# Reordering the opening of the row stage of a spectral-mixer training kernel, one forward bank from the other PSUM ring, and the last moves on three queues

## The chip, the cores and the metric

The kernel runs as one program on one core of a Trainium2 chip. The metric is device time in microseconds (us), the median of several executions; lower is better. A profile of one further execution gives every instruction's start and duration on the core's engines: PE (TensorE, matrix products; its weight loads are listed apart as PEld), DVE (VectorE), ACT (ScalarE), POOL (GpSimd) and SP (SyncE, which here only issues DMA transfers).

## The reference

The kernel computes the forward pass of one block and all its gradients (inputs and outputs bf16, x and grad_out [1, 2048, 448]):

```python
def _A_ref(x, w_r, w_i):                      # spectral filter
    X = rfft2(x.astype(float32), axes=(-2, -1))
    X = X * (w_r + 1j * w_i)
    return irfft2(X, s=(2048, 448), axes=(-2, -1)).astype(bfloat16)

def _B_ref(x, w1, b1, w2, b2):                # MLP over the 2048 tokens
    h = _layernorm(x)
    u = gelu(einsum("bsd,sf->bdf", h, w1) + b1)
    return (einsum("bdf,fs->bds", u, w2) + b2).transpose(0, 2, 1)

h  = x + _A_ref(_layernorm(x), w_r, w_i)
h2 = h + _B_ref(_layernorm(h), w1, b1, w2, b2)
out, vjp = jax.vjp(f, x, w_r, w_i, w1, b1, w2, b2);  grads = vjp(grad_out)
```

## The kernel before, in words

All work is in tiles of 128 partitions. Fourier transforms are matrix products with tables of sines that the kernel makes itself. The 2048 rows are split as 16 x 128: a *row stage* transforms the 128-long part of the rows and the 448 columns (`row_a`, `row_b`), a *spectral stage* (`s2_stage`) does the 16-long part forward, the filter, and the 16-long part back, and `inv_rows` goes back to rows and columns. The sections that the change touches lie in the first 95 us; the MLP, its gradients and the backward spectral pass follow.

**Order.** PE, SP, DVE and ACT run their instructions in the order in which the Python code emits them; POOL alone is ordered by the build. So what is emitted ahead of something on the same engine delays it.

**Weight-gradient matmuls as filling.** `dg_gen` (line 828) computes W2 @ grad_out: 14 blocks j of 16 matmuls (j, t), 128x448 each, into one `ps_mm` bank per block. `fill(n)` (792) emits n of them between other work; FILL_A and FILL_B (908, 909) say how many at each step t, and `drain()` the rest. Blocks 0 to 4 of W2 are turned on PE (`turn_w2`, 314): transposes into PSUM, copied out by ACT, called from inside `dg_gen` (block 4 after matmul (3, 4)); later blocks are turned by DMA.

**PSUM.** There are two rings of four banks, `ps_ff` (177) and `ps_mm` (180).

**Who copies out of PSUM.** `evac` (184) picks ACT or DVE by a running account of estimated work (`Meter`, 53; costs in lines 64 to 71).

**The row stage (871 to 951).** Layernorm statistics (`ln_stats`, 806) of the tiles of x; their reciprocal standard deviation by ACT's Sqrt and a DVE reciprocal (tiles 0 to 3), by nine small Newton steps on DVE (`rstd_of`, 849; tiles 4 and 5) or the like on POOL. `fold_prep` or `fold_quarters` fold a pair of tiles on DVE; `scale_R` puts the row's factor into the matrix R; `row_a(t)` (660) is four matmuls with it into one `ps_ff` bank, copied out to `blks`. `row_b(h)` (670) is four matmuls with the table `csF` into another bank; after each odd h a DMA, the *move*, lays the result out anew as D2. Step t runs `row_a(t + 1)`, then filling, `scale_R(t + 3)`, `row_b(t - 3)`, a fold, statistics, and steps of `gen_UV` (479), which makes the tables U and V.
`gen_RT` (523) makes R transposed by one matmul from four rearranged copies of R (903 to 907); `inv_rows` is its first user. `defer` (204) issues a DMA only after 1.1 us of PE work (RESH_LAG) have been emitted.

**The spectral stage (696).** Five rounds s. `four` (699) does 48 small matmuls into four banks: forward for s < 4, back for the round before. Forward results are copied by ACT, multiplied on DVE with the filter, transformed back, copied, and moved to D3 by DMA (730, 731); the last four moves gate `inv_rows` (756), whose `first` needs D3 and R transposed, and whose copies `aT` feed the second product. Its consumer `h_consumer` (988) forms h and its statistics.

**SP's queue.** It issues x, grad_out and W2 loads first (331 to 346), among them `gtail`, a tail of grad_out of 16 x 64, then two small bias loads (`load_biases`, 813), the filter's loads (`w_io`), the moves, and, after the spectral stage, the chunks of W2 and W1 for the MLP (1024 to 1028). `load_w1c` fills a ring of three; the third lies where W2's block 13 lay.

Of the kernel before, what the change touches and what calls it, by code (L numbers as in the profile page):

```python
# [124 lines left out]
def kernel(  # L125
# [188 lines left out]
    def turn_w2(j, parts=((0, 8), (8, 8))):  # L314
        for h, n in parts:
            pt = (ps_mm if j < 2 else ps_ff)()[:].bitcast(BF16).rearrange("p (t c) -> p t c", c=P)
            for t in range(n):
                nc.tensor.transpose(pt[:, t, :], w2n[j][:, h + t, :], ident[:])
            sc.copy(out=w2Ts[j][:, h:h + n, :], in_=pt[:, 0:n, :])
# [26 lines left out]
    nc.sync.dma_start(out=gtail[:, 0:64], in_=grad_out[0][S - 16:S, 3 * P:D])  # L346
# [261 lines left out]
    resh = [nc.sync]  # L608
# [51 lines left out]
    def row_a(t, R):  # L660
        pa = ps_ff()
        ft = folds[t // 2]
        for k in range(4):
            o = DC * (4 * (t % 2) + k)
            mm(pa[:, k * P:(k + 1) * P], lhsT=ft[:, o:o + P], rhs=R, start=True, stop=True)
        if t % 4 == 0:
            blks[t // 4] = blk_ring.next()
        evac(out=blks[t // 4][:, :, t % 4, :], in_=pa[:].rearrange("p (n x) -> p n x", x=8))

    def row_b(h, quarters=None):  # L670
        u, e, c = h // 4, h // 2 % 2, h % 2
        if h < 0 or h >= NT:
            return
        pd = ps_ff()
        pv = pd[:, 0:452].rearrange("p (c k) -> p c k", c=2)
        pq = pd[:, 0:452].rearrange("p (c e k) -> p c e k", c=2, e=2)
        for w in (1, 0):
            for b in range(2):
                n = 4 * (4 * (2 * w + b) + 2 * c + e)
                lhsT = blks[u][0:DC, n:n + 4].rearrange("p i j x -> p (i j x)")  # L680
                if quarters is not None:
                    mm(pq[:, 1 - w, b, :], lhsT=lhsT, rhs=quarters[0:DC, w, b, 0:KW // 2], start=True, stop=True)
                    continue
                mm(pv[:, 1 - w, :], lhsT=lhsT, rhs=csF[0:DC, w, b, :], start=(b == 0), stop=(b == 1))
        if c == 0:
            css[h // 2] = cs_ring.next()
        cs = css[h // 2]
        if quarters is not None:
            evac(out=cs[:, c].rearrange("p w (j e) -> p w e j", e=2), in_=pq)
        else:  # L690
            evac(out=cs[:, c], in_=pv)
        if c:
            defer(RESH_LAG, lambda: resh[0].dma_start(out=D2[u:u + 125:4, 8 * e:8 * e + 8].rearrange("p g c k -> p (g c k)"),
                                                      in_=cs.rearrange("p x c k -> p (x c k)")), cs)

    def s2_stage(get_x, on_mult, n1, n2, gap, after=None, scale=None, split=False):
        flush()

        def four(tables, s, turn, rhs):
            gs = set_groups(s)  # L700
            ps = [ps_ff()[:, 0:452].rearrange("p (c k) -> p c k", c=2) for _ in gs]
# [10 lines left out]
        for s in range(5):  # L712
# [8 lines left out]
            if s:  # L721
                for a, pv in enumerate(four((VTt, UTt, UTn), s - 1, -1, lambda a, g, r: y[blk(r), a])):
# [7 lines left out]
                    eng = nc.sync if split and s == 4 and a > 1 else gp_  # L730
# [82 lines left out]
    def load_biases():  # L813
        gp_.memset(smr, 0.0)
        nc.sync.dma_start(out=smr[0:NFB, 0, :], in_=B_b1.rearrange("(j p) -> j p", p=P))
# [88 lines left out]
    for c in range(2):  # L904
        for e in range(2):
            sc.copy(out=Rp.rearrange("p (e a q b c) -> p c e a q b", e=2, c=2, q=8, a=2)[:, c, e],
                    in_=Rm[:, 64 * c + 32 * e:64 * c + 32 * e + 32].rearrange("p (q a b) -> p a q b", q=8, a=2))
    FILL_A = (4, 4, 8, 12, 6, 3, 3, 3, 3, 3, 3, 3, 3, 3, 3, 3)
    FILL_B = (0, 0, 2, 2, 2, 2, 4, 4, 3, 2, 2, 2, 2, 2, 2, 2)
    for t in range(NT):  # L910
        if t == 0:
            load_w2T()
        if t + 1 < NT:
            row_a(t + 1, Rs.pop(t + 1))
        fill(FILL_A[t])
        if 1 <= t and t + 3 < NT:
            if t + 3 in (4, 8, 12):
                while Meter.side:
                    Meter.side.pop(0)()
            Rs[t + 3] = scale_R(t + 3)  # L920
# [28 lines left out]
        if t == 2:  # L949
# [11 lines left out]
    while held_w2:  # L961
        held_w2.pop(0)()
    fill(14)
# [6 lines left out]
    drain()  # L970
# [7 lines left out]

    assert not pending
# [8 lines left out]
    def h_consumer(s1, py):  # L988
# [3 lines left out]
        if s1 >= 1:  # L992
# [32 lines left out]
    w1cs = [load_w1c(jp) for jp in range(3)]  # L1025
# [426 lines left out]
```

## Time and profile before

| | us |
|---|---|
| runs | 342.69, 340.54, 342.59; median 342.59 |
| the profiled execution | 340.96 |
| its span, first to last instruction | 339.2 |
| PE idle in the span | 8.9 |
| granted TensorE clock | 0.999 |

Busy us by stretch, from the same profile (span's start is 0):

| stretch | PE | DVE | ACT | POOL |
|---|---|---|---|---|
| 6.47 to 19.35, opening up to row_b(0) | 11.25 of 12.88 | 12.12 | 11.11 | 9.95 |
| 19.35 to 32.84, up to row_a(10) | 12.36 of 13.49 | 13.17 | 9.27 | 7.07 |
| 32.84 to 49.20, end of the row stage | 16.36 of 16.36 | 10.39 | 11.42 | 5.86 |
| 49.20 to 76.11, spectral stage | 26.50 of 26.91 | 16.77 | 17.77 | 8.33 |
| 76.11 to 92.85, inverse rows | 16.34 of 16.74 | 13.10 | 15.47 | 3.82 |

How to read it: a timeline row gives start, duration, engine, source line, operation, the tile written and read, the form, and in brackets how long the engine was idle just before and what ended that. Most instructions are recorded by a helper, so L84 is any DVE or ACT operation, L220 a matmul, L225 a small one. A row merges equal neighbours (x4). A waits line gives engine and line, what it waited for, total us, times, longest. A windows line gives, for a stretch, its length, then the busy time of PE, PEld, DVE, ACT and POOL with the number of instructions, the granted clock, the DMA share and GB/s. Matmul ends are modelled, so "busy" can hide short waits between starts; a 448-column matmul that waits for nothing starts 0.187 us after the one before.

### The profile page before, as it was taken

The page shows a single profiled execution, that of the slowest core. Times are in us where ns is not written, and L with a number is a line of the kernel's source. Part 1 is how long each engine was busy: PE and PEld are TensorE (multiplying, and loading weights), DVE is VectorE, ACT ScalarE, POOL GpSimd, SP SyncE. Part 2 cuts the span into 40 slices and gives each one's busy share as a digit, 9 for nine tenths or more (in the row PEclk, how much of TensorE's full clock was granted, in tenths as well). Part 3 has the DMA queues.
Part 4 walks back from the last instruction along what each step waited for, and adds up shares of the span by engine and source line. Part 5 has one row for each costly group of instructions (what it writes and reads, how often), then busy time and mean ns, then how long its engine had stood idle before and what let it go on. Part 6 is the DMA issues. An engine that isn't in the chain of part 4 may idle for free.

```text
span 339.2 us, 7995 instructions
## 1 busy us (share of the span) xinstructions
PE 330.3 (97%) x2893; PEld 174.0 (51%) x2893; DVE 252.6 (74%) x678; ACT 206.2 (61%) x447; POOL 83.9 (25%) x255
## 2 busy tenths in 40 slices
PE   8898999999999999999999999999999999999995
PEld 4565665456545555555555555555334344555552
DVE  8999649726947888594226988787598984599994
ACT  6886766858965544523132346665488875688882
POOL 7755602331310000000001111210002222156660
PEclk9999999999999999999999999999999999999999
DMA  7979999949999999787986989636998999969785
GB/s 250 399 195 183 228 245 196 167 110 261 252 366 305 337 277 241 179 259 197 187 192 154 188 176 165 171 83 203 262 254 280 184 227 281 349 164 295 233 309 198
DMA packets 136142, 78.03 MB, mean 230 GB/s; under 512 B 86568, under 2 KB 127512, under 8 KB 135976
## 3 DMA queue, kind: packets, MB, share of 16 engines
q1 hardware_dynamic: 133576, 73.59, 82.6%
q0 software_dynamic: 2528, 3.95, 5.5%
q8 instruction: 22, 0.36, 0.5%
q14 instruction: 16, 0.13, 0.2%
HBM read 28.33 MB, written 22.04 MB: 149 GB/s over the span
## 4 chain that ended last, share of the span: by engine, by line
PE 85%; DVE 6%; ACT 3%; DMA 2%; SPq 2%; issue 1%; POOL 0%; DVEq 0%; ACTq 0%
PE ps_mm L220 73%; PE ps_ff L220 8%; PE ps_ff L225 4%; DMA rA<-in_A_x_dram 2%; ACT rO L84 2%; DVE r L84 2%; DVE stats L84 1%; SPq L329 1%; SPq L310 1%; DVE rS L84 1%; DVE rA L84 1%; ACT rAT L84 0%; DVE rD L84 0%; DVE rX L84 0%; DVE rB L84 0%
## 5 line engine op out<-in xcount | busy, mean ns | idle before, releaser
L220 PEld LDWEIGHTS <-r 128*128 128x128 bf16 (+2 forms) x628 | 58.4, 104 | 47.6 <-issue 3.0
L220 PEld LDWEIGHTS <-rS 128*128 128x128 bf16 (+1 forms) x468 | 36.3, 97 | 33.4 <-issue 7.7
L84 ACT CAST rO<-ps_mm 128x512 bf16<-128x512 f32 (+1 forms) x69 | 36.9, 584 | 14.6 <-PE ps_mm L220 13.0
L220 PE MATMUL ps_mm<-rD,r 128*128 128x448 bf16 x224 | 44.5, 352 | 0.0
L220 PEld LDWEIGHTS <-rst 128*128 128x128 bf16 (+1 forms) x320 | 23.6, 97 | 31.3 <-issue 14.0
L731 POOL DMA_DIRECT2D r<-r x30 | 17.8, 601 | 66.5 <-ACT r L84 59.3
L220 PE MATMUL ps_mm<-rC,rE 128*128 128x448 bf16 x144 | 32.1, 353 | 0.5 <-DMA rC<-in_grad_out_dram 0.4
L220 PE MATMUL ps_mm<-rB,r 128*128 128x448 bf16 x160 | 31.2, 352 | 0.1
L220 PE MATMUL ps_mm<-rG,rst 128*128 128x512 bf16 (+1 forms) x128 | 28.7, 380 | 0.2 <-ACT rO L84 0.2
L220 PE MATMUL ps_mm<-r,rst 128*128 128x512 bf16 (+2 forms) x144 | 27.4, 345 | 0.0
L84 ACT ACTIVATE r<-ps_mm,rstd_h 128x448 bf16<-128x448 f32 x16 | 10.1, 633 | 26.8 <-PE ps_mm L220 26.8
L84 ACT CAST r<-ps_ff 128x452 bf16<-128x452 f32 x43 | 23.2, 589 | 4.5 <-PE ps_ff L225 2.1
L84 DVE SCALAR_TENSOR_TENSOR r<-ps_mm,b2col,r 128x448 bf16<-128x448 f32 x16 | 10.9, 682 | 19.9 <-PE ps_mm L220 19.8
L84 ACT ACTIVATE r<-rC 128x448 bf16<-128x448 bf16 x16 | 9.1, 571 | 26.7 <-DMA out_dram<-r 14.1
L1189 POOL TENSOR_SCALAR lcol<-lcol 128x1 f32<-128x1 f32 x16 | 8.5, 528 | 64.7 <-ACT r L84 64.7
L84 ACT ACTIVATE rG<-rG 128x896 bf16<-128x896 bf16 x14 | 13.3, 950 | 14.9 <-DVE rG L84 14.7
L220 PEld LDWEIGHTS <-rO 128*128 128x128 bf16 (+1 forms) x165 | 15.3, 98 | 12.2 <-ACT rO L84 0.2
L84 ACT CAST rS<-ps_ff 128x512 bf16<-128x512 f32 x31 | 18.1, 587 | 2.5 <-PE ps_ff L220 2.4
L220 PE MATMUL ps_ff<-csI,rAT 113*128 113x224 bf16 (+1 forms) x108 | 19.0, 298 | 0.4 <-ACT rAT L84 0.2
L84 DVE TENSOR_SCALAR rG<-rG 128x896 bf16<-128x896 bf16 x28 | 10.9, 388 | 10.0 <-ACT rG L84 10.0
L220 PE MATMUL ps_mm<-rC,rO 128*128 128x448 bf16 x80 | 18.1, 353 | 0.0
L84 ACT CAST rG<-ps_mm 128x512 bf16<-128x512 f32 (+1 forms) x28 | 13.8, 534 | 6.8 <-PE ps_mm L220 6.7
(202 smaller groups left out, 638.2 us busy)
## 6 DMA issues: line engine op xcount, KB each, us to landing
out_dram<-rO SPq DMA_DIRECT2D x34, 256.0 KB, 3.0
r<-in_B_w_dram SPq DMA_DIRECT2D x5, 1024.0 KB, 8.4
r<-r POOLq DMA_DIRECT2D x30, 113.0 KB, 5.4
out_dram<-rG SPq DMA_DIRECT2D x11, 256.0 KB, 3.7
r<-r SPq DMA_DIRECT2D x12, 226.0 KB, 2.5
r<-in_B_w_dram SPq DMA_DIRECT2D x3, 896.0 KB, 5.1
rS<-in_B_w_dram SPq DMA_DIRECT2D x3, 896.0 KB
rB<-in_B_w_dram SPq DMA_DIRECT2D x5, 512.0 KB, 9.8
```

What stands on the lines that cost most here:

```text
L84: fn(**kw)
L220: nc.tensor.matmul(out, lhsT=lhsT, rhs=rhs, start=start, stop=stop)
L225: nc.tensor.matmul(out, lhsT=lhsT, rhs=rhs, start=start, stop=stop)
L310: nc.sync.dma_start(out=w2n[j], in_=B_w2[j * P:(j + 1) * P, :].rearrange("f (t c) -> f t c", c=P))
L329: nc.sync.dma_start(out=go_tp[:, 4 * q:4 * q + 4, :], in_=go_tp_d[:, 4 * q:4 * q + 4, :])
L731: defer(RESH_LAG, lambda g=g, ab=ab, eng=eng: eng.dma_start(out=D3[rowbase(g):rowbase(g) + 29:4, :, :, :], in_=ab), ab)
L1189: gp_.tensor_scalar(out=m1, in0=ms, scalar1=-1.0 / D, scalar2=None, op0=ALU.mult)
```

## The change

In the opening: the statistics and Sqrt of tiles 2, 3 are emitted ahead of the first W2 copies; row_a(0) to row_a(3) are run before the loop and copied by ACT whatever the account says, the latter two late (`late_a`); tiles 4, 5 take Sqrt and reciprocal in place of the Newton steps, with their fold and scalings right behind; the sine of the forward table comes before the loop. In the loop: row_a(8) is copied by ACT, the second copy of W2's block 4 comes after it (`late_c`); one step of `gen_UV` is taken before the statistics of t = 1 and none at t = 6; R transposed is made at t = 13, not t = 2. The last row move goes at once on ACT's DMA queue. The gtail and bias loads go behind the row stage. In the spectral stage the fourth bank of each forward group is a `ps_mm` bank; the last four D3 moves go on POOL, SP, ACT, SP (before: POOL, POOL, SP, SP). After it 18 filling matmuls are run in place of all the rest, so that the last of them stand in `inv_rows`, and the third W1 chunk is loaded from `h_consumer`.

```diff
-            sc.copy(out=w2Ts[j][:, h:h + n, :], in_=pt[:, 0:n, :])
+            (Later(sc, late_c) if j == 4 and h else sc).copy(out=w2Ts[j][:, h:h + n, :], in_=pt[:, 0:n, :])
...
-    nc.sync.dma_start(out=gtail[:, 0:64], in_=grad_out[0][S - 16:S, 3 * P:D])
...
-    def row_a(t, R):
+    def row_a(t, R, how=None):
...
-        evac(out=blks[t // 4][:, :, t % 4, :], in_=pa[:].rearrange("p (n x) -> p n x", x=8))
+        (how or evac)(out=blks[t // 4][:, :, t % 4, :], in_=pa[:].rearrange("p (n x) -> p n x", x=8))
...
         if c:
-            defer(RESH_LAG, lambda: resh[0].dma_start(...), cs)
+            eng = nc.scalar if h == NT - 1 and quarters is csQ else nc.sync
+
+            def move():
+                eng.dma_start(...)
+            if eng is nc.scalar:
+                move()
+            else:
+                defer(RESH_LAG, move, cs)
...
-            ps = [ps_ff()[:, 0:452].rearrange("p (c k) -> p c k", c=2) for _ in gs]
+            ps = [(ps_mm if split and turn > 0 and a == 3 else ps_ff)()[:, 0:452].rearrange("p (c k) -> p c k", c=2)
+                  for a in range(4)]
...
-                    eng = nc.sync if split and s == 4 and a > 1 else gp_
+                    eng = (gp_, nc.sync, nc.scalar, nc.sync)[a] if split and s == 4 else gp_
...
     def load_biases():
         gp_.memset(smr, 0.0)
+        nc.sync.dma_start(out=gtail[:, 0:64], in_=grad_out[0][S - 16:S, 3 * P:D])
...
-    turn_w2(0, ((0, 4), (4, 4)))
-    row_a(0, Rs.pop(0))
     for t in range(2, 4):
         ln_stats(xn, t, mvx)
     sc.activation(out=rstd_x[:, 2:4], in_=mvx[:, 2:4, 1], func=ACT.Sqrt, bias=eps_x, scale=1.0)
+    turn_w2(0, ((0, 4), (4, 4)))
+    row_a(0, Rs.pop(0), sc.copy)
     turn_w2(0, ((8, 8),))
+    row_a(1, Rs.pop(1), sc.copy)
     fold_prep(xn, 1)
+    ve.reciprocal(out=rstd_x[:, 2:4], in_=rstd_x[:, 2:4])
+    Rs.update({t: scale_R(t) for t in range(2, 4)})
+    late_a, late_c = [], []
     cs_ops = []
     gen_fwd_d(cs_ops)
-    ve.reciprocal(out=rstd_x[:, 2:4], in_=rstd_x[:, 2:4])
-    Rs.update({t: scale_R(t) for t in range(2, 4)})
...
-    fill(4)
+    fill(3)
+    for t in range(2, 4):
+        row_a(t, Rs.pop(t), Later(sc, late_a).copy)
+    fill(1)
     for t in (4, 5):
         ln_stats(xn, t, mvx)
-    for fn in rstd_of(4, 6):
+    sc.activation(out=rstd_x[:, 4:6], in_=mvx[:, 4:6, 1], func=ACT.Sqrt, bias=eps_x, scale=1.0)
+    fold_prep(xn, 2)
+    ve.reciprocal(out=rstd_x[:, 4:6], in_=rstd_x[:, 4:6])
+    Rs.update({t: scale_R(t) for t in range(4, 6)})
+    sc.activation(out=warm, in_=half_r, func=ACT.Sin, scale=1.0 / 64.0)
+    cs_ops.pop(0)()
+    for fn in late_a:
         fn()
-    fill(0)
-    turn_biases, place_biases = load_biases()
...
-    for c in range(2):
-        for e in range(2):
-            sc.copy(out=Rp.rearrange(...)[:, c, e], in_=Rm[:, 64 * c + 32 * e:64 * c + 32 * e + 32].rearrange(...))
...
+    def uv_step():
+        for _ in range(3):
+            if next(uv, None):
+                break
...
-        if t + 1 < NT:
-            row_a(t + 1, Rs.pop(t + 1))
+        if 4 <= t + 1 < NT:
+            row_a(t + 1, Rs.pop(t + 1), sc.copy if t == 7 else None)
+        if t == 7:
+            late_c.pop()()
         fill(FILL_A[t])
-        if 1 <= t and t + 3 < NT:
+        if 3 <= t and t + 3 < NT:
...
         if t % 2 and t < 12:
-            if t // 2 + 2 < 2 * U_Q:
+            if t == 1:
+                pass
+            elif t // 2 + 2 < 2 * U_Q:
...
         if t == 1:
-            sc.activation(out=warm, in_=half_r, func=ACT.Sin, scale=1.0 / 64.0)
             while cs_ops:
                 cs_ops.pop(0)()
+            uv_step()
         for i in STATS.get(t, ()):
             ln_stats(xn, i, mvx)
-        for _ in range(3 if t > 0 else 0):
-            if next(uv, None):
-                break
+        if t not in (0, 1, 6):
+            uv_step()
...
-        if t == 2:
+        if t == 13:
+            for c in range(2):
+                for e in range(2):
+                    sc.copy(out=Rp.rearrange(...)[:, c, e], in_=Rm[:, 64 * c + 32 * e:64 * c + 32 * e + 32].rearrange(...))
             gen_RT()
...
     while held_w2:
         held_w2.pop(0)()
+    turn_biases, place_biases = load_biases()
     fill(14)
...
-    drain()
+    fill(18)
...
-    assert not pending
...
-        if s1 >= 1:
+        if s1 == 0:
+            w1cs.append(load_w1c(2))
+        else:
             square_h(s1 - 1)
...
-    w1cs = [load_w1c(jp) for jp in range(3)]
+    w1cs = [load_w1c(jp) for jp in range(2)]
```

More of the change, by code (lines that the diff above doesn't have):

```diff
@@ L606 @@
     D3 = cut(r3, 0, NT, 2, KW)
-    resh = [nc.sync]
     def rowbase(s_):
@@ L692, in row_b @@
         if c:
-            defer(RESH_LAG, lambda: resh[0].dma_start(out=D2[u:u + 125:4, 8 * e:8 * e + 8].rearrange("p g c k -> p (g c k)"),
-                                                      in_=cs.rearrange("p x c k -> p (x c k)")), cs)
+            eng = nc.scalar if h == NT - 1 and quarters is csQ else nc.sync
+            def move():
+                eng.dma_start(out=D2[u:u + 125:4, 8 * e:8 * e + 8].rearrange("p g c k -> p (g c k)"),
+                              in_=cs.rearrange("p x c k -> p (x c k)"))
+            if eng is nc.scalar:
+                move()
+            else:
+                defer(RESH_LAG, move, cs)
     def s2_stage(get_x, on_mult, n1, n2, gap, after=None, scale=None, split=False):
@@ L903 @@
     W_AT = {0: 2, 1: 1, 2: 2, 3: 1, 4: 2, **{t: 1 for t in range(5, 11)}, 11: 4}
-    for c in range(2):
-        for e in range(2):
-            sc.copy(out=Rp.rearrange("p (e a q b c) -> p c e a q b", e=2, c=2, q=8, a=2)[:, c, e],
-                    in_=Rm[:, 64 * c + 32 * e:64 * c + 32 * e + 32].rearrange("p (q a b) -> p a q b", q=8, a=2))
     FILL_A = (4, 4, 8, 12, 6, 3, 3, 3, 3, 3, 3, 3, 3, 3, 3, 3)
     FILL_B = (0, 0, 2, 2, 2, 2, 4, 4, 3, 2, 2, 2, 2, 2, 2, 2)
+    def uv_step():
+        for _ in range(3):
+            if next(uv, None):
+                break
     for t in range(NT):
@@ L948 @@
             gen_inv_s(INV_S[t])
-        if t == 2:
+        if t == 13:
+            for c in range(2):
+                for e in range(2):
+                    sc.copy(out=Rp.rearrange("p (e a q b c) -> p c e a q b", e=2, c=2, q=8, a=2)[:, c, e],
+                            in_=Rm[:, 64 * c + 32 * e:64 * c + 32 * e + 32].rearrange("p (q a b) -> p a q b", q=8, a=2))
             gen_RT()
```

## The prediction

> **What bounds the kernel now.** I read the page first (busy shares, chain of waits), then the waits of the tensor engine, then the timelines of the stages that the diff touches.
>
> ```profile
> span 339.2 us, 7995 instructions
> PE 330.3 (97%) x2893; PEld 174.0 (51%) x2893; DVE 252.6 (74%) x678; ACT 206.2 (61%) x447; POOL 83.9 (25%) x255
> PE 85%; DVE 6%; ACT 3%; DMA 2%; SPq 2%; issue 1%; POOL 0%; DVEq 0%; ACTq 0%
> ```
>
> PE is busy for 97%, and no matmul is removed. All that can be won is time in which PE waits: 8.9 us idle, plus waits that hide inside modelled "busy" time. The profiled execution took 340.96 us (span 339.2 and 1.8 around it), 1.63 below the median of 342.59; I sum against it and add the difference back.
>
> The waits of PE in the first 46 us, and the rows around the two long ones:
>
> ```profile
> PE ps_ff L220 <- DVE rS L84: 1.8, 2, 1.0
> PE ps_mm L220 <- DMA rC<-in_grad_out_dram: 0.4, 1, 0.4
> PE ps_mm L318 <- DMA rB<-in_B_w_dram: 0.3, 1, 0.3
> ```
> ```profile
> 14.26 0.54 PE L220 MATMUL ps_mm<-rC,rE 128*128 128x448 bf16 x2
> 15.57 0.65 PE L220 MATMUL ps_ff<-rX,rS 128*128 128x128 bf16 x4 [0.78 <-DVE rS L84]
> ...
> 28.88 0.92 PE L220 MATMUL ps_mm<-rC,rO 128*128 128x448 bf16 x4
> 30.81 0.38 PE L220 MATMUL ps_ff<-rX,rS 128*128 128x128 bf16 x4 [1.01 <-DVE rS L84]
> ```
> ```profile
> 12.01 0.18 DVE L84 TENSOR_SCALAR mvx<-mvx 128x2 f32<-128x2 f32 x1
> ...
> 13.64 0.16 DVE L84 SCALAR_TENSOR_TENSOR rstd_x<-nt_f,rstd_x 128x2 f32<-128x2 f32 x1
> ...
> 15.13 0.69 DVE L84 TENSOR_TENSOR rS<-rA 128x448 bf16<-128x448 bf16 x2
> ...
> 30.08 0.68 DVE L84 CAST rS<-ps_ff 128x512 bf16<-128x512 f32 x1
> ```
>
> row_a(4) (15.57) waits for the fold at 15.13, which stands behind nine tiny Newton steps (12.01 to 13.80: 1.79 us). row_a(9) (30.81) waits for the copy of row_a(8), late on a full DVE (13.17 us busy of the 13.49 between 19.35 and 32.84). 448 columns pass in 0.187 us back to back, so the true losses are the starts less that: 1.2 us at row_a(4) (0.25 of it inside the group), 1.18 at row_a(9), 0.28 at row_a(10).
>
> **The opening, part by part.** *ACT.* The Sqrt of tiles 2, 3 now stands ahead of the first W2 copies and waits for statistics that end at 7.56. By the start-to-start times of its rows (0.48 us for 512 elements, 0.93 for 1024) the copies follow at 7.76, and the first weight-gradient matmul goes from 8.19 to 8.38. row_a(1)'s copy also comes before the copies of the second W2 block; that block's first copy ends at 11.2, so matmuls (1, 0..3) start there, not at 10.48. Most of this is covered: the next group waits anyway for the second quarter of grad_out (landed 11.67). It starts at 11.97 rather than 11.71, and with row_a(2), row_a(3) and the RT product out of the way (0.22, 0.22, 0.06) matmul (1, 4) starts at 12.72 against 12.69.
> *DVE.* Nine Newton steps go (-1.79 us), a reciprocal comes (0.16), Sqrt goes to ACT, and fold 2 and both scalings come directly behind the statistics: ready at 13.5. Ten matmuls after 12.72, row_a(4) starts at 14.6 instead of 15.57, without its inner 0.25: -1.2. The third W2 block lands at 15.29, so its transposes wait 0.1. The planner's balance (costs of lines 64 to 71, summed by hand; for the kernel before it gives the split that the trace shows) now sends row_b(0)'s copy to DVE, behind which row_b(1) finds its bank 0.2 late. Opening: -1.0 (bounds +0.3, if ACT's longer queue shows in full, and -1.2).
> *Late copies.* row_a(2) and row_a(3) keep their two banks until ACT has done Sqrt, Sin table (1.28) and the first basis: to about 15.7. row_a(4) and the next transposes still find the banks of row_a(0) and (1); cost nothing, 0.9 us if a bank is missing (one 1024 copy).
>
> **The middle.** Three table steps (17.73 to 19.43 before) now run on DVE while x's third quarter is in flight (landed 16.42), so with the Newton steps gone DVE is 1.2 us ahead at t = 3. row_a(8) goes to ACT (0.6 off DVE), and the sine of V, which ACT awaited for 2.76 us with the W2 copies behind it, comes one step later. So row_a(9) waits no more; the second fold behind row_a(10) ends 1.2 + 0.6 earlier, at 31.0, while PE could be there at 30.2. row_a(10): 32.84 to 31.0, so **-1.8** for all up to here. Bounds: -1.0 (opening alone) and -2.8 (DVE no longer last).
>
> **The RT product** moves to t = 13, behind four copies that ACT does only after the copy of the inverse table:
>
> ```profile
> 11.65 0.60 ACT L84 COPY rO<-Rm 128x32 bf16<-128x32 bf16 x4
> ```
> ```profile
> 41.52 0.37 ACT L84 CAST UVT<-ps_ff 128x256 bf16<-128x256 f32 x1 [0.51 <-PE ps_ff L225]
> ```
>
> Before, this lay 2 us ahead of its use. Now the copies end at 41.52 + 0.3 + 0.6 = 42.4, and PE, in order, stands at the product from 41.34 with two W2 matmuls and row_a(15) queued behind it: **+1.05** (0.3 if the table's copy goes to DVE, 1.3 with a slower hand-over). No cover: PE is the last engine here.
>
> **The end of the row stage.** The last move goes to ACT's queue at once (some 0.6 us of ACT, as an issue on SP; the csI copies behind it have 1.5 us of room). The planner puts row_b(12) and (13) both on ACT, so the move that the first spectral group needs (issued 44.98, landed 49.00, group at 49.20) is some 0.4 late: **+0.2** (0 to 0.5). Three tiny loads leave SP's early queue, so the W2 and filter loads behind them are issued earlier; those in front land as before: 0. In their new place they delay W2 transposes by about 1 us of 5 us room: 0.
>
> **The spectral stage.** Widths of the eight groups of small matmuls; the narrowest is the floor:
>
> ```profile
> 49.20:49.91 0.71, 0.71 (x50) 0.51 (x49) 0.00 (x0) 0.00 (x0) 0.00 (x0) 1.00 0.91 199
> 60.39:61.32 0.93, 0.93 (x50) 0.53 (x49) 0.83 (x3) 0.71 (x2) 0.00 (x0) 1.00 1.18 266
> 65.45:66.74 1.29, 0.94 (x49) 0.42 (x49) 1.19 (x4) 0.65 (x2) 0.00 (x0) 1.00 0.87 153
> ```
>
> Five groups exceed 0.71: by 0.19, 0.18, 0.22, 0.19 and 0.58. In each, the matmul of the fourth bank starts just after ACT's fourth copy of the group before (58.17 after 58.13). With a forward bank from the other ring each group needs only three copies, done 0.43 earlier and before the group starts. 0.78 goes, and 0.1 to 0.2 of the 0.58, whose rest ends in "issue": **-0.9** (-0.3 to -1.3).
>
> **Into the inverse rows.**
>
> ```profile
> 76.09 0.53 ACT L84 CAST rD<-ps_mm 128x448 bf16<-128x448 f32 x1 [2.50 <-PE ps_mm L220]
> 76.11 0.85 PE L220 MATMUL ps_ff<-RTm,r 128*113 128x128 bf16 x12
> 76.55 1.07 ACT L84 CAST rAT<-ps_ff 113x512 bf16<-113x512 f32 x2
> 77.19 0.93 PE L220 MATMUL ps_ff<-csI,rAT 113*128 113x448 bf16 x4 [0.23 <-ACT rAT L84]
> ```
>
> PE ended its weight matmuls at 75.89, waited for the last D3 move (landed 75.97), then for aT's copy behind that of rD. Two of the 20 matmuls now stand after the three products, so PE is free at 75.51, and rD's copy comes later and (same balance) on DVE, which idles here. The last move is issued 0.4 earlier (SP's first of its two is now the one whose copy ends at 71.27, not 71.60, and POOL's second issue of 0.60 goes): landed 75.6, aT copied 76.6, next product 76.65: **-0.5** (-0.15 if the landing stays; -0.6). The rows after this are ACT's (10.00 busy of 10 from 80 to 90); ACT starts 0.5 earlier too, so the gain holds.
> A rule against it: the Trainium skill, "DMA: Bandwidth & Descriptors", section "Issuing engines are not separate DMA queues", says that DMAs from several engines share the same 16 DMA engines and that spreading them saves only the issue time. By it the sum would be 0.35 less; the landings before (73.97, 74.86, 75.64, 75.97) lie close enough for that.
>
> Sum: -1.8 + 1.05 + 0.2 - 0.9 - 0.5 = -1.95, so 339.0 for a profiled run and **340.6** as median.
>
> **Rivals.**
> - *The row stage gives more* (0.18): DVE is not last, the opening's DMA waits go with the rest, -2.8 - 0.6 in all; with +1.05, -0.9, -0.5: -3.75, 338.8. For: the window is only just full of DVE. Against: the fold chain has no slack.
> - *The opening's gain stays on ACT* (0.20): four forced copies and a table load make ACT what DVE was; -1.0 instead of -1.8 before row_a(10), so -1.15: 341.4. For: ACT is 11.11 busy of 12.88 from 6.47 to 19.35.
> - *The last landing stays at 75.97* (0.14): -0.15 for -0.5, so -1.6: 341.0. It is the skill's rule named above as a mechanism of this stage.
> - *The change does not free the bank* (0.05): DVE or the weight ring holds the fourth bank, the 0.9 stays: 341.5.
> - *The third W1 chunk binds* (0.07): it is now issued behind two transposes (5.36 us) and two W2 loads (1.48) on SP, at 88 instead of 81.58, with two loads of 896 KB ahead in the queue. Needed at 105.50 before, 103.5 now; I expect it at 99. It decides from 103.5: late by one more landing time of such a load (8.4 us) it comes at 107, PE stands 3.5 us, net +1.55: 344.1, slower.
> - The forecast itself: 0.36.
>
> **How the numbers follow.** 1% (3.4 us) is about what a measurement tells from no change. Faster by more needs the first rival, 0.18, and a little tail of the forecast: 0.19. Slower by more than 1% needs the last rival at a higher price, or a wait that no row shows: 0.06. The rest, 0.75, is within. The three runs before spread over 2.1 us, so the range goes from 338.4 (below the first rival) to 343.0 (above all but the last).
>
> **What would show it.** Right: row_a(4) near 14.6 and no idle PE before row_a(9); a hole of about 1 us in PE near 39.5 to 41, ended by ACT's copies of Rm; all but one of the six middle groups at 0.71 to 0.75; no ACT copy of rD ahead of the first rAT. Wrong: a hole before matmuls (1, 0..3) longer than 0.8 us; PE idle at the first spectral group; a wait for rO near 103. The forecast falls if the RT product finds its copies done.

## The result, and the profile after

The changed kernel takes 340.15 us (median of 22 runs, 339.42 to 341.85), the kernel before 341.25 (22 runs on the same chip, 340.36 to 343.96): a ratio of 0.9965, 95% interval 0.9949 to 0.9982. That is a gain of 1.1 us, real but within 1%. The profiled execution took 340.7 us. Medians below count every execution, but ratios and intervals leave out those more than 1.5% above the fastest of the same kernel: one each in e3, e4 and e8, three in e12, five in e9, and in e1 the profiled one (span 559.6 us at a mean clock of 0.56), so that e1 has no profile to read.

The page of the changed kernel, first lines and chain:

```profile
span 338.6 us, 7976 instructions
PE 327.8 (97%) x2884; PEld 174.2 (51%) x2893; DVE 252.3 (75%) x671; ACT 206.0 (61%) x447; POOL 85.3 (25%) x254
PE 71%; DVE 1%; ACT 1%; issue 0%
```

The span is 0.6 us shorter (339.2 before). PE is 97% busy as before, with 10.8 us idle in place of 8.9 (some matmul records are missing, so this is rough). PE's waits (engine, line, what it waited for: total us, times, longest):

```profile
PE ps_ff L220 <- ACT rO L84: 1.0, 1, 1.0
PE ps_ff L225 <- DMA r<-rX: 1.0, 1, 1.0
PE ps_mm L220 <- ACT rE L84: 0.9, 2, 0.5
PE ps_ff L220 <- DMA r<-r: 0.6, 1, 0.6
PE ps_ff L220 <- DVE rS L84: 0.5, 1, 0.5
```

The wait for the fold (DVE rS) fell from 1.8 us to 0.5. Two of 0.52 and 0.37 for ACT's copies of W2 (ACT rE) came in the opening, where the waits for grad_out and W2 went. Three others are new: for the copies of Rm (ACT rO), for a row move in front of the first spectral group (DMA r<-rX), for the last D3 move (DMA r<-r). In PE's timeline (start, duration, operation, idle time before and its end):

```profile
14.82 0.39 PE L220 MATMUL ps_ff<-rX,rS 128*128 128x128 bf16 x4
...
31.27 0.40 PE L220 MATMUL ps_ff<-rX,rS 128*128 128x128 bf16 x4 [0.54 <-DVE rS L84]
...
40.85 0.23 PE L220 MATMUL ps_ff<-ident,rO 128*128 128x128 bf16 x1 [1.02 <-ACT rO L84]
...
49.80 0.58 PE L225 MATMUL ps_ff<-r,Vt 32*32 32x452 bf16 x12 [0.96 <-DMA r<-rX]
```

The row of row_a(10) before:

```profile
32.84 0.40 PE L220 MATMUL ps_ff<-rX,rS 128*128 128x128 bf16 x4
```

row_a(10) starts 1.57 us earlier than before (31.27 for 32.84), the RT product loses 1.02, and the first spectral group still starts 0.60 *later* (49.80 for 49.20): in this execution all that the opening won is gone there. The windows of three of the spectral groups (stretch, its length, busy PE, PEld, DVE, ACT, POOL, clock, DMA share, GB/s):

```profile
49.80:50.51 0.71, 0.71 (x48) 0.59 (x48) 0.00 (x0) 0.00 (x0) 0.00 (x0) 1.00 0.76 170
60.77:61.48 0.71, 0.71 (x50) 0.49 (x49) 0.67 (x2) 0.67 (x2) 0.00 (x0) 1.00 1.32 385
65.41:66.12 0.71, 0.71 (x49) 0.49 (x49) 0.61 (x3) 0.68 (x2) 0.00 (x0) 1.00 1.36 382
```

All groups are now 0.71 to 0.73 wide, the former 1.29 too. From the first group to the last it is 19.45 us, 20.67 before. The last group's window, before and after:

```profile
69.87:70.58 0.71, 0.71 (x49) 0.49 (x49) 0.00 (x0) 0.00 (x0) 0.16 (x1) 1.00 0.67 175
69.25:69.96 0.71, 0.71 (x50) 0.49 (x49) 0.00 (x0) 0.00 (x0) 0.10 (x1) 1.00 0.59 179
```

The entry to the inverse rows, PE and ACT:

```profile
75.62 0.85 PE L220 MATMUL ps_ff<-RTm,r 128*113 128x128 bf16 x12 [0.57 <-DMA r<-r]
76.06 1.07 ACT L84 CAST rAT<-ps_ff 113x512 bf16<-113x512 f32 x2 [1.83 <-PE ps_ff L220]
76.70 0.93 PE L220 MATMUL ps_ff<-csI,rAT 113*128 113x448 bf16 x4
```

The second product starts at 76.70, 0.49 earlier; behind it PE is busy in both kernels and the difference stays.

### The profile page after: what moved, and what is told of

Read it like the earlier page. It is cut to its first block, busy times and chain, and to the rows that moved or that the text cites. A ratio compares the mean times of both kernels' runs of the same rounds, so it can differ in the third digit from the quotient of the medians.

```text
span 338.6 us, 7976 instructions
## 1 busy us (share of the span) xinstructions
PE 327.8 (97%) x2884; PEld 174.2 (51%) x2893; DVE 252.3 (75%) x671; ACT 206.0 (61%) x447; POOL 85.3 (25%) x254
## 4 chain that ended last, share of the span: by engine, by line
PE 71%; DVE 1%; ACT 1%; issue 0%
PE ps_mm L220 64%; PE ps_ff L220 6%; PE ps_ff L225 2%; DVE rA L84 1%; ACT rO L84 1%; DVE rB L84 0%; ACT rAT L84 0%; ACT rC L84 0%; DVE rG L84 0%; ACT rstd_h L84 0%; DVE rstd_h L84 0%
## 5 line engine op out<-in xcount | busy, mean ns | idle before, releaser
L220 PE MATMUL ps_mm<-rG,rst 128*128 128x512 bf16 (+1 forms) x121 | 26.9, 380 | 1.0 <-issue 0.8
L220 PEld LDWEIGHTS <-rE 128*128 128x128 bf16 x144 | 12.8, 98 | 10.4 <-ACT rE L84 1.2
```

The source lines that it names most:

```text
L220: nc.tensor.matmul(out, lhsT=lhsT, rhs=rhs, start=start, stop=stop)
```

## The experiments

The reading so far became theory T: the row stage ends in a *join*, where PE meets the moves of D2. What PE wins before the join is given back as a wait; from the first spectral group on, the chain has a fixed length, which only the bank swap shortened. Rivals were that PE's order decides (then the hole at RT is worth 1 us), and that every part pays a little. Ratios are to the kernel before, run on the same chip beside each experiment, with 95% intervals.

**e1, the last row move back on SP.**

```diff
-            eng = nc.scalar if h == NT - 1 and quarters is csQ else nc.sync
+            eng = nc.sync
```

> The changed kernel with the last row move back on SP, deferred as before. Theory A (two queues share the DMA engines: the move of row_b(13), which the first spectral group needs, is slowed by the last move that ACT's queue sends beside it): that move lands 3.5 us after its issue instead of 4.3, PE's wait at the first spectral group falls from 1.0 to about 0.3 us, time 0.6 to 0.7 us below the changed kernel. Theory B (the two copies in a row on ACT make the move late): the wait stays at 0.9 or more and the time is the same. Theory C (SP's backlog of filter loads sets when the moves land, whatever PE and ACT do): the wait stays or grows by the 0.6 that SP spends on the extra issue.

Measured: 341.0 us, ratio 0.9983 (0.9949 to 1.0017). It can't be told from the changed kernel nor from the kernel before: if this part matters, it is by less than these runs tell apart, and the wait that the theories speak of was not seen.

**e2, the four copies of Rm two steps ahead of the RT product.**

```diff
-        if t == 13:
+        if t == 11:
             for c in range(2):
                 for e in range(2):
-                    sc.copy(...)
+                    nc.scalar.copy(...)
+        if t == 13:
+            for _ in range(4):
+                load[0] += sc.cost('copy', 32, True)
...
             gen_RT()
```

> The changed kernel with the four rearranged copies of R emitted at t = 11; the product stays at t = 13. Theory A: the hole of 1.02 us before the product goes; the move of row_b(13) comes earlier by as much, so the wait at the first spectral group stays near 1.0 and the time falls by 0.9 to 1.0 us. Theory C (the moves land when SP and the DMA engines let them): the hole goes, the wait at the first spectral group grows to 2.0, and the time is the same within 0.2 us.

The account of `evac` is charged for the copies at t = 13 as before, so no other copy changes its engine. Measured: 340.99 us, ratio 0.9981 (0.9952 to 1.0011). In PE's timeline:

```profile
39.13 0.23 PE L220 MATMUL ps_ff<-ident,rO 128*128 128x128 bf16 x1
...
49.71 0.51 PE L225 MATMUL ps_ff<-r,Vt 32*32 32x452 bf16 x12 [2.58 <-DMA r<-rX]
```

The hole at RT is gone, PE reaches the join 1.71 us earlier, and waits there 1.62 us longer. SP issued the move of row_b(13) at 43.20, 1.68 earlier than in the changed kernel, and it landed at 49.57 where it had landed at 49.67. (Of the 1.71 us, 1.02 are the hole; most of the rest is an opening that ran 0.63 faster in this execution, row_a(10) at 30.64.) A move is 16 parts that land one by one: 15 of them were there by 48.41 here and by 48.40 in the changed kernel, and the last one at the times given. So in these two profiles neither PE nor the issue sets the landing, and the wait of the changed kernel, where PE stood ready at 48.84, is for one part out of 16.

**e3, three repairs at once**: the edits of e1 and e2, and the copies of row_b(12) to (15) alternately on DVE and ACT.

```diff
-            evac(out=cs[:, c].rearrange("p w (j e) -> p w e j", e=2), in_=pq)
+            ({12: ve.tensor_copy, 13: sc.copy, 14: ve.tensor_copy, 15: sc.copy}.get(h, evac) if quarters is csQ else evac)(
+                out=cs[:, c].rearrange("p w (j e) -> p w e j", e=2), in_=pq)
```

> The changed kernel with the copies of R at t = 11, the last row move on SP, and row_b(12), (13), (14), (15) copied by DVE, ACT, DVE, ACT as in the kernel before. Theories A and B together: no hole before the product, wait at the first spectral group 0.2 us or less, 1.7 to 2.0 us below the changed kernel. Theory C: 0 to 0.5 below.

Measured: 340.31 us, ratio 0.9981 (0.9949 to 1.0013). The profile has a 2.05 us wait at the join (group at 50.20), and then something new. Windows:

```profile
48.01:51.43 3.42, 1.37 (x52) 0.91 (x52) 0.00 (x0) 0.48 (x2) 0.00 (x0) 1.00 1.32 197
51.43:54.84 3.41, 3.41 (x11) 1.35 (x10) 2.47 (x5) 1.38 (x4) 0.00 (x0) 0.50 0.87 193
54.84:58.25 3.41, 3.41 (x78) 1.62 (x91) 2.62 (x6) 1.75 (x5) 0.00 (x0) 1.00 0.80 165
```

The third number from the end is the granted clock: from 51.43 to 54.84 TensorE ran at half of it. The weight-gradient matmuls of that stretch take 0.37 us each in place of 0.187, and the second group comes 5.59 us after the first, not 3.90 as in e2.

**e4, the fourth bank from `ps_ff` again**; the rest of the change stays.

```diff
-            ps = [(ps_mm if split and turn > 0 and a == 3 else ps_ff)()[:, 0:452].rearrange("p (c k) -> p c k", c=2)
+            ps = [ps_ff()[:, 0:452].rearrange("p (c k) -> p c k", c=2)
                   for a in range(4)]
```

> The changed kernel with all four forward banks from the first ring again. If the bank swap is what brought all eight groups of the spectral stage to 0.71 us, five of them go back to 0.85 to 0.95 and the time rises by 0.8 to 1.0 us. If they were shortened by the late start of the stage instead (copies on ACT have more room), they stay at 0.71 and the time is the same.

Measured: 342.03 us, ratio 1.0016 (0.9983 to 1.0049), an interval that just fails to meet that of the full change (0.9949 to 0.9982). Windows, and PE's row of the first group:

```profile
48.32:49.29 0.97, 0.97 (x49) 0.70 (x49) 0.74 (x3) 0.03 (x1) 0.00 (x0) 1.00 1.27 187
59.76:60.63 0.87, 0.87 (x49) 0.54 (x48) 0.77 (x3) 0.66 (x2) 0.00 (x0) 1.00 1.21 162
64.77:65.81 1.04, 0.96 (x50) 0.44 (x50) 0.94 (x4) 0.65 (x2) 0.00 (x0) 1.00 0.79 141
```
```profile
48.32 0.73 PE L225 MATMUL ps_ff<-r,Vt 32*32 32x452 bf16 x16
```

The wide groups are back, and first to last group takes 20.60 us. Without the swap the runs show no gain.

The row stage of e4 is that of the changed kernel, and yet its first group starts at 48.32 without a wait, 1.48 us earlier: the move was issued at 44.32 and landed at 48.18, 3.86 us later, where the changed kernel's profile has 4.79 us. So T's join does not take back everything in every execution.

**e5, the bank swap alone**, on the kernel before: the diff of e4 the other way round.

> The kernel before with one edit: the fourth bank of each forward spectral group from the second to the last comes from the ring ps_mm; opening, RT product, moves and everything else as before. Theory (the row stage ends in a join on DMA, so the rest of the change gives back there what it gains): the widened groups (.90, .89, .93, .90, 1.29) become .71 to .75, the first matmul of the inverse rows (76.11 before) starts near 75.2, and the time is 0.8 to 1.1 us below the kernel before, which is the whole gain of the change. Rival (the opening pays too, and the bank swap is one of several equal parts): 0.3 to 0.5 us below. Second rival (the third bank of the second ring is missed by the weight-gradient matmuls): groups narrow, but the weight matmuls between them wait, and the time is the same.

Measured: 341.28 us, ratio 0.9992 (0.9956 to 1.0028). The profile shows the mechanism (all groups 0.71 to 0.73, 19.31 us from first to last, 0.57 less at the first product of the inverse rows), but the time is nearer to the rival's 0.3 us than to T's 0.8 to 1.1; the interval holds both, and no gain at all. That the swap alone makes the whole gain is not shown.

**e6 and e11, the imaginary half of the filter not loaded** (on e2; left out: those loads; a memset puts zeros there, so the filter multiplies by its real half). The memset of `Wc[:, 1]` stands inside `w_io` in e6; in e11 the other two, behind the row loop, take its place:

```diff
+            if c_ and not store:
+                gp_.memset(Wc[:, 1], 0.0)
+                moves = []
...
+    gp_.memset(Wc[:, 1, 0:8], 0.0)
+    gp_.memset(Wc[:, 1, 8:16], 0.0)
     gp_.memset(csF[:, 0, :, 0:1], 1.0)
```

> Built on e2_copies_early. It leaves out the loads of the imaginary half of the spectral filter (about 1 MB in rows of 450 bytes); that half is set to zero by one memset on GpSimd instead, so the filter multiplies by its real half only; no other work changes. Theory (what is queued on the DMA engines in front of the moves sets when they land, and so when the first spectral group starts): the move of row_b(13) lands 1 to 3 us earlier than 49.57, the wait of 2.6 us before the first spectral group shrinks to 0 to 1.5, the DMA share between 32.84 and 49.8 falls from 1.1 to 0.8 or less, and the time falls by 1 to 2.5 us against e2 (to about 338.5 to 340). Rival 1 (the moves themselves are slow, 4 us from issue to landing whatever else is in flight): the landing stays within 0.3 of 49.6 and so do wait and time. Rival 2 (the spectral stage is bound by VectorE's products): the group starts earlier, but the first matmul of the inverse rows stays near 75.6.

> e6_no_imag with its flaw mended: the imaginary half of the spectral filter is again not loaded (left out) and set to zero on GpSimd, but by two memsets behind the row loop, so that nothing of the row stage waits for them (in e6 the memset, 3.11 us at 32.96, stood in front of GpSimd's Newton steps and TensorE waited 6.3 us for row_a(11)). Theory: with some 1 MB less in front of the moves the move of row_b(13) lands by 46.5, the wait of 2.6 us before the first spectral group falls to under 0.5, the group starts at 47.1 to 47.6, and the time is 2 to 2.6 us below e2 (about 338.5). Rival (the moves' own rate): landing near 49.6, same time.

Measured: 347.0 us, 1.0179 (1.0125 to 1.0234), and 347.39 us, 1.0178 (1.0149 to 1.0207). Neither tested what it was meant to, and for the same reason. POOL's order is the build's: the memset came ahead of Newton steps in e11 too, and waited for filter loads. POOL's timeline of e11:

```profile
33.44 1.60 POOL L987 MEMSET rW<- 128x1800 bf16 x1 [5.62 <-DMA rW<-in_A_w_r_dram]
34.97 1.61 POOL L988 MEMSET rW<- 128x1800 bf16 x1
36.53 0.20 POOL L410 TENSOR_TENSOR nt_f<-rstd_x 128x2 f32<-128x2 f32 x1
```

row_a(11) waited 6.8 us for the scaling behind those steps. What the run still shows is the moves on DMA engines that had little to do (share 0.12 between 45 and 50 us). The DMA lines of e2, then of e11 (count, KB each, median us from issue to landing):

```profile
r<-rX SPq DMA_DIRECT2D x3, 226.0 KB, 5.9
```
```profile
r<-rX SPq DMA_DIRECT2D x3, 226.0 KB, 2.8
```

With little in front the moves took about half the time. The comparison is rough, since e11 issued them 5 to 10 us later, in another surrounding.

**e7, the last four filter loads behind the row stage** (on e2).

```diff
-    W_AT = {0: 2, 1: 1, 2: 2, 3: 1, 4: 2, **{t: 1 for t in range(5, 11)}, 11: 4}
+    W_AT = {0: 2, 1: 1, 2: 2, 3: 1, 4: 2, **{t: 1 for t in range(5, 11)}}
```

> Built on e2_copies_early. The last four filter loads on GpSimd's queue are issued after the row stage (with the rest of the loads that are left over) in place of in its twelfth step; nothing is left out. Theory as in e6: the moves land up to 1.5 us earlier, the wait of 2.6 us before the first spectral group shrinks, the time is 0.5 to 1.5 us below e2 if the four loads still land before VectorE multiplies by them; if they don't, the products of the first set wait for them and it is given back (same time). Rival (the moves' own rate sets the landing): nothing moves by more than 0.3 us.

Measured: 346.48 us, 1.0133 (1.009 to 1.0175). PE at the join, then DVE:

```profile
48.36 0.51 PE L225 MATMUL ps_ff<-r,Vt 32*32 32x452 bf16 x12 [1.24 <-DMA r<-rX]
```
```profile
56.72 0.63 DVE L84 TENSOR_TENSOR rS<-rX,rW 128x900 bf16<-128x900 bf16 x1 [5.99 <-DMA rO<-in_B_w_dram]
```

The move landed 1.34 us earlier (48.23), as T said, with the issue at 43.34, near e2's 43.20; 15 of its 16 parts were there by 46.22, 2.2 us earlier than in e2. But two of the loads, issued at 44.64 and 45.11, landed at 55.82 and 56.25, behind a W2 transpose issued at 44.01 (landed 56.46), and DVE's first product waited for them 6 us, longer than T or its rival had allowed for. Behind that wait and PE's own TensorE ran at half clock from 58.61 to 65.43, so part of the loss is the clock.

**e8, five weight-gradient matmuls moved from behind the spectral stage to before it** (on e2).

```diff
-    fill(14)
+    fill(19)
...
-    fill(18)
+    fill(13)
```

> Built on e2_copies_early. Five weight-gradient matmuls (0.94 us) that stood behind the spectral stage stand before it: fill(14) becomes fill(19), fill(18) becomes fill(13). Theory (both joins wait for DMA, PE has slack at each): the wait before the first spectral group shrinks from 2.6 to about 1.7 us with the group at the same 49.7, the first matmul of the inverse rows starts at the same 75.6 behind a wait that is longer by about 0.9 us; time the same within 0.3 us. Rival (PE's order is what counts): the first spectral group starts 0.9 us later and the time is up by 0.3 to 0.9 us.

Measured: 340.94 us, 0.9975 (0.9949 to 1.0002). PE's timeline:

```profile
48.87 0.44 PE L225 MATMUL ps_ff<-r,Vt 32*32 32x452 bf16 x12
...
74.60 0.85 PE L220 MATMUL ps_ff<-RTm,r 128*113 128x128 bf16 x12 [1.58 <-DMA r<-r]
```

0.94 us more of PE work ahead of the join cost nothing, and the wait at the D3 moves grew by 1.0 us. The move landed at 48.66 here. Up to the move this is e2's code, so its landing differs by execution: 4.63 us after its issue here, 6.37 in e2's profile.

**e9 and e10, one W2 transpose held back until the moves are issued.** e9 is the changed kernel with the first edit alone; e10 is e2 with all.

```diff
-CAP = 9
+CAP = 8
...
-    fill(14)
+    fill(8)
...
-    fill(18)
+    fill(24)
```

> The changed kernel with one number changed: CAP = 8 for 9. The DMA transpose of W2's block 8 (in the changed kernel issued on SP at 36.07, landed 43.50, first used by a weight-gradient matmul just behind the first spectral group, 50.5 to 51.3) is held back until the moves of the row stage are issued; nothing is left out. Theory (the moves stand behind 4 us of transfers that were issued before them, and their landing starts a chain of fixed length, 25.8 us from the first spectral group to the first matmul of the inverse rows): the move of row_b(13) lands 1.5 to 3.5 us earlier than 49.67, the wait of 0.96 us before the first spectral group goes, the group starts near 48.8; the time is 0.5 to 1.0 us below the changed kernel (339.1 to 339.7 where that has 340.15). Rival 1 (a move takes 4 us from issue to landing by itself): landing and group within 0.3 of 49.7, same time. Rival 2 (the held transpose binds): a wait for rO behind the first spectral group, group 2 late, time the same or up to 1.5 us longer.

> e2_copies_early (copies of Rm two steps early) with CAP = 8, and six weight-gradient matmuls moved from in front of the spectral stage to behind it (fill(14) becomes fill(8), fill(18) becomes fill(24)); nothing is left out. Theory as in e9: TensorE is through with what stands before the first spectral group at about 46.0, the move of row_b(13) lands at 46 to 47.5, so the group starts 2 to 3.5 us earlier than 49.71; 25.8 us later, at 72 to 73.5 in place of 75.5, the inverse rows begin, and the time is 338.0 to 339.0 against 341.2 for the kernel before (ratio 0.990 to 0.994). Rival 1 (landing unchanged): group near 49.7, longer wait (3.7 us), time up by 0 to 1 us against e2. Rival 2 (the held transpose binds): a wait of 1 to 2 us for rO between the first spectral groups, time within 0.5 us of e2.

Measured: e9 345.01 us (343.01 without the five longest), 1.0043 (1.0007 to 1.008); e10 343.69 us, 1.0055 (1.0029 to 1.0081): both above what T and its rivals gave. PE's timeline of e10:

```profile
47.74 0.50 PE L225 MATMUL ps_ff<-r,Vt 32*32 32x452 bf16 x12 [0.67 <-DMA r<-rX]
...
66.61 0.32 PE L225 MATMUL ps_ff<-rS,UTn 32*32 32x226 bf16 x15 [2.46 <-issue]
...
78.66 0.85 PE L220 MATMUL ps_ff<-RTm,r 128*113 128x128 bf16 x12 [1.36 <-DMA r<-r]
```

The join came 1.97 us earlier than in e2, the move landing 3.3 us after its issue. But every later W2 transpose moved back (SP issued one from 61.98 to 67.45), the D3 moves stood among them (the last landed 8.5 us after the last group began, 6.2 in the changed kernel), and the inverse rows began 3.0 us later than in the changed kernel. The largest single loss in between is the hole of 2.46 us at 66.61, for which the profile names no cause ("issue"). In e9 PE had no wait at the join, as T said (group at 49.24, the move there at 48.62), but one wait for W2 behind it took 6.5 us in its profiled execution, which at 350.95 us is one of the longest.

**e12, the last four filter loads on SP, behind the moves and ahead of the next transpose** (on e2).

```diff
-            late = [m for n, m in enumerate(moves) if n in (0, 2, 4, 6)] if c_ and not store else []
+            late = []
...
-    W_AT = {0: 2, 1: 1, 2: 2, 3: 1, 4: 2, **{t: 1 for t in range(5, 11)}, 11: 4}
+    W_AT = {0: 2, 1: 1, 2: 2, 3: 1, 4: 2, **{t: 1 for t in range(5, 11)}}
...
+    flush()
     for _ in w_loads:
         pass
```

> e2_copies_early with the last four filter loads behind the moves of the row stage, all on SP's queue and in front of the next W2 transpose (in e7 they were on GpSimd's queue and two of them landed behind that transpose, at 55.8 and 56.3); the order of the nine loads of the imaginary half is the natural one. Nothing is left out. Theory (what is issued ahead sets when the moves land, what is issued behind them does not): the move of row_b(13) lands near 48.2 in place of 49.57, the group starts near 48.4, the four loads land by 50.5, about when VectorE's first product could start (50.2), and the inverse rows start 0.5 to 1.2 us before 75.5; time 339.8 to 340.6 where e2 had 340.99. Rival 1 (moves' own rate): nothing moves, same time as e2. Rival 2 (the loads land late, or the later W2 transposes, 1 to 2 us later on SP, make the D3 moves wait as in e10): a wait of VectorE for the filter or a hole in front of the last spectral groups, 0.5 to 4 us slower than e2.

Measured: 342.29 us, 1.0007 (0.9977 to 1.0038): nothing won. PE's timeline and the window behind it:

```profile
51.78 0.51 PE L225 MATMUL ps_ff<-r,Vt 32*32 32x452 bf16 x12 [4.67 <-DMA r<-rX]
```
```profile
51.78:54.00 2.22, 2.22 (x52) 1.18 (x53) 0.00 (x0) 1.42 (x4) 0.00 (x0) 0.59 0.83 188
```

Of the 16 parts of row_b(13)'s move 15 had landed by 47.87, 0.5 us earlier than in e2, the last at 51.64. Why one part lags by 3.8 us stayed open; T, which gave 48.2 for the landing, did not foresee it. The clock dropped again, to 0.59.

**The clock in the single executions** shows a second price of longer waits, beside the landing. Executions with a mean granted clock below 0.997, and medians:

| kernel | executions | below 0.997 | median of these | median of the others |
|---|---|---|---|---|
| before (beside e1 to e4) | 35 | 4 | 344.97 | 341.24 |
| changed | 22 | 0 | | 340.15 |
| e1, without the disturbed one | 11 | 0 | | 340.92 |
| e2 | 12 | 5 | 342.33 | 339.75 |
| e3 | 12 | 5 | 342.12 | 339.96 |
| e4 | 12 | 2 | 345.98 | 341.83 |
| e5 | 12 | 2 | 344.97 | 341.18 |
| e7 | 6 | 6 | 346.48 | |
| e8 | 12 | 1 | 345.12 | 340.89 |
| e9 | 12 | 6 | 349.02 | 342.50 |
| e10 | 12 | 7 | 344.13 | 341.74 |
| e12 | 12 | 5 | 346.49 | 341.07 |

Where the clock holds, e2 is 0.4 us below the changed kernel (seven executions, 338.94 to 341.32, so not settled); in 5 of 12 it loses 2.2. That the drop lies at the join is seen in the profiles of e3 and e12; for e2's own low executions, which have e3's mean clock (0.994, 0.995), it is inferred. The kernel before, e4, e5 and e8 have a few low executions as well, at 344 to 348 us, so not every drop comes from a long wait at the join.

## Why the prediction was right, and where its steps were wrong

The time fell within 0.5 us of the forecast and the change stayed within 1%, but the sum behind it was too good: -1.95 us were forecast, the profile's span gives -0.6 and the runs -1.1. The forecast was taken from a median of three runs (342.59) that lies 1.3 above the median of 22; that made up for the difference. The nearness of the number is luck in part: from the median of 22 the same sum gives 339.3.

| term | forecast | profile |
|---|---|---|
| opening and middle, to row_a(10) | -1.8 | -1.57 |
| RT product | +1.05 | +1.02 |
| end of the row stage | +0.2 | +1.15 |
| spectral stage | -0.9 | -1.22 |
| into the inverse rows | -0.5 | +0.13 |
| sum | -1.95 | -0.49 |

- *Opening and middle*: right in mechanism and nearly in size. row_a(4) at 14.82 (14.6 forecast), row_a(9) without a wait, row_a(10) at 31.27 (31.0). DVE is still last there. Eleven profiles with this opening have row_a(10) between 30.62 and 31.74, the two with the old one (before, e5) at 32.84 and 33.23, so a single row here is good to about 0.5 us.
- *RT product*: right, by the copies behind ACT's other work. What it is worth was taken wrong: "PE is the last engine here" held only until the moves were last. e2 took the hole away, and no gain showed in the time.
- *End of the row stage*: the mis-sized term, +1.15 for +0.2 in the changed kernel's profile (49.80 less 49.20, with the 1.57 won and the 1.02 lost put back). The step took the move's landing to follow its issue by the 4.0 us of the kernel before, and PE to be there no earlier than the move. The issue came out as forecast: 0.45 late against PE (44.88 for 44.98, where PE had won 0.55), 0.4 forecast. The flight, from issue to landing, did not: 4.79 us, so the move landed 0.67 later than before, and PE stood there at 48.84. "PE idle at the first spectral group", a sign of being wrong that the prediction named, came. But it is no fixed price of the change. In e4's profile, with the same row stage, the flight is 3.86 us and the term comes to +0.23 (48.32 less 49.20, with 2.13 won and 1.02 lost put back); which of the two is usual, two profiles can't say. What makes the flight longer is, as far as shown, the load on the DMA engines: their share between 32.84 and the join was 1.12 in the changed kernel, 1.05 in e4 and 1.04 before; e2 issued 1.68 earlier for the same landing; e7 took transfers away in front and the move came earlier; e10 and e11 had shorter flights with fewer transfers ahead. e12 fits for 15 of the 16 parts and not for the last, at 51.64. Why one part comes so late is open.
- *Spectral stage*: right, and larger. "0.1 to 0.2 of the 0.58, whose rest ends in issue" was wrong: that group went from 1.29 to 0.71, in e5 too, where only the bank changed. e4 without the swap brings widths of 0.87 to 1.04 back.
- *Into the inverse rows*: wrong in all three parts. The two matmuls behind the products only became a wait of 0.57. The copy of rD went to DVE as forecast (76.89), but it had delayed nothing: first product to second is 1.08 us in both kernels. And the last D3 move lands no earlier with three queues: measured from the start of the last group it is 6.10 and 6.51 us with two (before, e5), 6.20 to 6.60 with three (changed, e2, e3, e4, e8). The rule that the prediction weighed (the Trainium skill, "DMA: Bandwidth & Descriptors", "Issuing engines are not separate DMA queues") held, so the rival built on it was right as a mechanism.
- *The other rivals*: the third W1 chunk was issued at 88.95 and landed at 100.3, ahead of its use, with no wait; the bank was freed; DVE stayed last at row_a(10), so the row stage did not give more, and ACT did not take the opening's gain.

Where the 1.1 us come from: the swap is needed (e4). In the profiles it shortens the way from the first spectral group to the inverse rows wherever that group starts: 25.7 to 26.2 us with it (changed, e2, e5, e6, e8, e11; more only where a clock drop, a wait for W2 or the filter, or another hole came in between), 26.9 and 27.3 without (before, e4). How much of the row stage's gain comes on top depends on when the last part of the move lands: the first group was 0.60 us later than before in the changed kernel's profile, 0.88 earlier in e4's. Whether the swap alone would give the 1.1 us (e5) is not settled.

## What to carry to other kernels

Where a stage ends in a join of an engine and transfers, look at what is queued on the DMA engines in front of the last transfer before counting a gain of the engine: an earlier issue can be worth nothing (1.68 us earlier here, the same landing), and a transfer moved behind the join must still find its place among the later ones. One profile of a join is one draw: the same code gave a landing 3.9 and 4.8 us after the issue. The price of a hole is not its length alone: two of 1 us left the clock as it was, one of 2 us or more could cost about 2 us on top. Count a moved matmul as won only where no wait stands behind its old place.

## What the hardware showed that was not expected

- *The clock drops after holes of 2 us, in steps of 3.41 us.* In or after waits of 2.05 (e3), 4.67 (e12), 6.53 (e9) and 6.81 us (e11), and in e7 among waits of 2.60 and 1.25, TensorE went to half rate; after 2.58 us in e2's profile, 2.46 in e10's and 0.96 and 1.02 in the changed kernel it did not. The half rate lasted 3.41 us in e3 (51.43 to 54.84) and e12 (52.19 to 55.61), 6.83 in e7 and e9, 10.24 in e11: one, two and three times the same step. The stretches at full rate ahead of them are whole multiples too (44.37 us in e3 is 13 steps), so the rate changes on a grid of such steps, whose place differs by execution. In e3 the whole hole lies in one step (48.01 to 51.43, with 0.8 us of small 32-row matmuls behind it). In e2's profile, counted back from the change of the clock at 339.11, a step ends at 48.98, inside the hole; PE is idle for 1.86 us of one step and 0.73 of the next:

```profile
45.57:48.98 3.41, 1.55 (x9) 0.59 (x6) 2.18 (x9) 0.94 (x4) 0.00 (x0) 1.00 1.55 327
48.98:52.39 3.41, 2.68 (x59) 1.63 (x60) 0.94 (x2) 1.85 (x4) 0.00 (x0) 1.00 0.72 166
```

  That the place of the grid decides is inferred from these; it would explain why a hole trips the clock in 5 of 12 executions of e2 only. Idle time alone does not decide: in e11 a step with 1.74 us of it (33.05 to 36.46) was enough. The Trainium skill, "TensorE: Matmul & The Clock Gate", "Part 1: The HAM clock gate", gives half rate after an idle window of about 3.4 us that runs freely. The length and the free place agree with these traces; but a window that was idle for 2.05 of its 3.41 us (e3) was enough here.
- *One transfer of 226 KB takes 2.2 to 6.5 us from issue to landing*: 2.2 in e11 (47.48 to 49.72) with few transfers ahead, 6.5 in e2 for the last move, which was alone on ACT's queue while SP's moves stood ahead of it.
- *One of the 16 parts of a move can come long after the others*: for row_b(13)'s move 0.7 (e9) to 3.8 us (e12) after the 15th, in ten of thirteen profiles; the group that reads the result waits for it.
- *Loads beside a W2 transpose can be held up*: two issued on POOL 0.6 and 1.1 us after it landed with it, 11 us after their issue (e7).
